# The last network's second weight as a scaled pair of fp16 parts, in four of five chunks

## The chip, the cores and the metric

The kernel is one program on one core of a Trainium2 chip. The metric is the device time of one execution in microseconds (us). The core has five engines with a queue each that is worked through strictly in order: PE (matrix products), DVE (vector), ACT (scalar functions), POOL (GpSimd) and SP (here it issues DMAs); they meet through semaphores only. Matrix products write to PSUM, everything else lies in SBUF.

## The reference

```python
attn = softmax(causal(q @ k.T / 8 + decay(f))) @ v          # 4 x 8 heads, 576 tokens, 64 wide
h = relu(attn @ w_in);  u, v = halves(h)                    # first network: 512 -> 2 x 512
x = (u * (w_spatial @ layernorm(v) + b_spatial)) @ w_out    # "moe"
xk = mu_k * x + (1 - mu_k) * previous_token(x)              # last network: "moe2"
xr = mu_r * x + (1 - mu_r) * previous_token(x)
k = relu(xk @ w_k)                                          # 512 -> 1024
out = sigmoid(xr @ w_r) * ((k * k) @ w_v)                   # 1024 -> 512
```

All is float32 with 2304 tokens in all. The weights arrive as 8-byte numbers and are converted to float32 on the chip.

## The kernel before, in words

Every float32 operand of a product is cut into a high and a low part, and a product is three matrix multiplications (`T3`: high x high, high x low, low x high) that add up in PSUM. Most operands are cut into **scaled fp16 parts**: a power of two is found from the operand's size (squares on ACT, a sum over all partitions by a small product with a matrix of ones on PE, named `tot`, and a few one-column instructions on DVE in `pow2`), ACT multiplies and rounds to the high part, and one SCALAR_TENSOR_TENSOR on DVE makes the low part. The second weight of the last network (`moe2_w_v`) and its operand, the squares `k2`, are cut without a scale into **two fp32r parts** (`split`: an ACT cast, a DVE subtraction).

The first 395 us are attention and the first network. What follows is the stage of the change: the 2304 tokens in five chunks (four of 512, the last of 256). Chunk by chunk there are, on PE, with names as in the code and line 927 of `mm` for all of them:

- `m3`: 4 groups of 12 matmuls (w_out), for the next chunk; ACT writes `x2` (L897), POOL copies one column across the chunk's edge (L899);
- `mix`: no PE; ACT (L947, L957) and DVE (L949, L958) make the fp16 parts `xx0`, `xx1` of xk and xr;
- `m4(fc)`, fc 0 to 7: 12 matmuls each (w_k, fp16); then ACT takes the relu out of PSUM (L976), DVE squares it (L977), ACT and DVE cut the square into fp32r parts (L65, L66);
- `m5(fc)`: 12 matmuls (4 groups of 128 tokens x 3), w_v as the moving operand, `k2` as weights, adding into four PSUM banks over all eight fc;
- `m6(j)`: 12 matmuls for each group of 128 tokens (w_r, fp16); ACT takes the sigmoid (L996).

At the end DVE multiplies the sums by the sigmoids (L1002) and SP writes the result out (L1004). Within `chunk`, m5 runs two steps behind m4: m4(fc), m5(fc-2); then the four m6, then m5(6) and m5(7). m4, m3, m6 and the `tot` products share four PSUM banks.

The order in each engine's queue is not the order of the code: a scheduler with a timing model of its own lays the queues out when the program is built, so a change of code moves instructions of several engines. `side` in `body` hands the next chunk's m3 and mix in between the steps of a chunk; `wrest` does the same with the loading and converting of weights.

Of the kernel before, what the change touches and what calls it, by code (L numbers as in the profile page):

```python
# [7 lines left out]
F32 = mybir.dt.float32  # L8
# [31 lines left out]
def f32(ap):  # L40
    return ap.bitcast(F32)


class K:
# [705 lines left out]
    def early_norms(self):  # L750

        nc, p = self.nc, self.p3
        self.ws = self.p3.tile([128, 4], F32, name="ws")
        wq = p.tile([128, 2, 4], F32, name="wq")
        self.gate_load(0)
        for n, nm in enumerate(("moe2_w_k", "moe_w_out")):
            for kc in range(4):
                self.sumsq(wq[:, n, kc:kc + 1], self.we[nm, kc, 0], self.junk2[:, 0:512])
                if kc % 2:
                    yield  # L760
        for x in range(2):
            self.gate_sums(0, x)
        self.gate_load(1)
        yield
        for x in range(2):
            self.gate_sums(1, x)
        yield
        w = p.tile([128, 2], F32, name="wt")
        nc.vector.tensor_reduce(w, self.total(wq.rearrange("p n k -> p (n k)"), 8).rearrange("p (n k) -> p n k", n=2), AX.X, ALU.add)
        with self.tc.high_priority(PRIO):  # L770
            self.pow2(self.ws[:, 0:2], w, 1e-12, 15)
            self.gsum(0)
            self.mixing_norms()
            self.gsum(1)
        yield
# [29 lines left out]
    def weights2(self, p, names, stage, pin=False):  # L805
# [5 lines left out]
        blocks = []  # L811
        for nm in names:
            rows, cn = a[nm].shape
            self.w2[nm] = p.tile([128, 2, rows // 128, cn], F16 if nm in SCALED else F32R, name=nm)
            blocks += [(nm, kc, slice(c0, c0 + 512)) for c0 in range(0, cn, 512) for kc in range(rows // 128)]

        ready = [x for x in blocks if (x[0], x[1], x[2].start) in self.we]
# [133 lines left out]
    def mix_parts(self, i, w, kc):  # L951
# [5 lines left out]
        nc.scalar.mul(hi, tmp[:, 0:n], sc)  # L957
        nc.vector.scalar_tensor_tensor(self.xx[w][:, 1, kc, 0:n], tmp[:, 0:n], sc, hi, ALU.mult, ALU.subtract)  # L958

    def chunk(self, i):  # L960
        nc, p = self.nc, self.p2
        t0, n = self.chunks[i]
        xk, sx = self.xx[0], self.sx3[i]
        wk, wr, wv = [self.w2["moe2_w_" + x] for x in "krv"]
# [5 lines left out]
        def m4(fc):  # L970
            ps = self.ps3.tile([128, 512], F32, tag="p", bufs=4, name="m4")
            self.mm(ps[:, 0:n], [(wk[:, ws, kc, 128 * fc:128 * fc + 128], xk[:, s_, kc, 0:n]) for kc in range(4) for s_, ws in T3])
            tmp = p.tile([128, 512], F32, tag="tmp", bufs=3, name="tmp")
            t = k2[fc] = p.tile([128, 2, 512], F32R, tag="k2", bufs=4, name="k2")
            u = 2 + 2 * (fc // 4)
            nc.scalar.activation(tmp[:, 0:n], ps[:, 0:n], AF.Relu, scale=sx[:, u:u + 1])  # L976
            nc.vector.tensor_tensor(tmp[:, 0:n], tmp[:, 0:n], tmp[:, 0:n], ALU.mult)  # L977
# [23 lines left out]
        for j in range(J):  # L1001
            nc.vector.tensor_tensor(o[j], o[j], acc[j], ALU.mult)  # L1002
            r0 = t0 + 128 * j
            nc.sync.dma_start(self.out.rearrange("b s d -> (b s) d")[r0:r0 + 128, :], o[j])  # L1004
        yield


def body(tc, a, out):
# [66 lines left out]
    for w in range(2):  # L1075
        for _ in k.mix(0, w):
# [2 lines left out]
            k.late_part()  # L1079
            next(wrest, 0)  # L1080
    for i in range(5):
        lg = k.gates(i + 2) if i < 2 else iter(())
        side = (x for y in ((m3[i + 1], k.mix(i + 1, 0), k.mix(i + 1, 1)) if i < 4 else ()) for x in y)
        n = 0
        for _ in k.chunk(i):
            if not i:
                k.late_part()
            next(wrest, 0)
            n += 1
            if n > 5:  # L1090
                next(lg, 0)
            if n <= 5 and i or n >= 9:
                next(side, 0)
            if n == 12:
                next(side, 0)
        for _ in side:
            next(wrest, 0)
    for p in (k.ps3, k.p2, wst, k.p3, wp, k.hl, k.c):
        p.release()


# [42 lines left out]
```

## Time and profile before

| | |
|---|---|
| median of 3 runs | 692.7 us (687.59, 692.7, 693.89) |
| the profiled execution's own time | 688.2 us |
| its span, first to last instruction | 686.5 us |
| busy: PE, DVE, ACT, POOL | 90%, 63%, 67%, 28% |
| mean granted TensorE clock | 0.981 |

The busy share is an average over stages; the span in 40 slices shows PE filled to nine tenths or more in nearly every slice after the first few, and POOL busy in the first half alone. Times in the trace count from the span's first instruction. A matmul's duration in the trace overlaps with the next one's: the price of one in a stream is the step from start to start.

### The profile page before, as it was taken

The page shows a single profiled execution, that of the slowest core. Times are in us where ns is not written, and L with a number is a line of the kernel's source. Part 1 is how long each engine was busy: PE and PEld are TensorE (multiplying, and loading weights), DVE is VectorE, ACT ScalarE, POOL GpSimd, SP SyncE. Part 2 cuts the span into 40 slices and gives each one's busy share as a digit, 9 for nine tenths or more (in the row PEclk, how much of TensorE's full clock was granted, in tenths as well). Part 3 has the DMA queues.
Part 4 walks back from the last instruction along what each step waited for, and adds up shares of the span by engine and source line. Part 5 has one row for each costly group of instructions (what it writes and reads, how often), then busy time and mean ns, then how long its engine had stood idle before and what let it go on. Part 6 is the DMA issues. An engine that isn't in the chain of part 4 may idle for free.

```text
span 686.5 us, 11120 instructions
## 1 busy us (share of the span) xinstructions
PE 616.0 (90%) x3720; PEld 368.8 (54%) x3720; DVE 435.8 (63%) x1238; ACT 462.4 (67%) x1022; POOL 189.7 (28%) x421
## 2 busy tenths in 40 slices
PE   0458686998988999989999799999999999999997
PEld 0123343566645566456667544565555556566584
DVE  6776857888578866685237978997328624532341
ACT  4678899898879978689339699885328334442531
POOL 7343444665446743475106010000000000000000
PEclk9998789999999999999999999999999999999999
DMA  7984632826763455441046582313001100100010
GB/s 236 233 220 105 166 87 59 233 48 165 191 143 106 109 138 128 103 90 32 19 146 213 178 283 70 123 62 123 0 1 32 62 1 0 62 1 0 1 62 32
DMA packets 69344, 69.75 MB, mean 102 GB/s; under 512 B 46659, under 2 KB 47395, under 8 KB 69286
## 3 DMA queue, kind: packets, MB, share of 16 engines
q1 hardware_dynamic: 68854, 67.85, 35.3%
q10 hardware_dynamic: 432, 1.18, 0.4%
q8 instruction: 29, 0.48, 0.3%
q14 instruction: 29, 0.24, 0.1%
HBM read 43.61 MB, written 9.55 MB: 77 GB/s over the span
## 4 chain that ended last, share of the span: by engine, by line
PE 66%; DVE 12%; DMA 10%; ACT 4%; SPq 3%; POOL 3%; issue 2%; DVEq 0%; POOLq 0%; ACTq 0%
PE m L927 42%; PE m L615 5%; PE o L393 4%; PE t L352 4%; PE s L298 4%; PE m1u L598 4%; DVE sx L309 3%; DMA qA<-qT 3%; PE m1v L530 3%; DMA qT<-nq 2%; SPq L341 2%; ACT junka L321 1%; DMA wst<-in_moe_w_k_dram 1%; DMA kT<-nk 1%; DMA qA<-mr 1%
## 5 line engine op out<-in xcount | busy, mean ns | idle before, releaser
L321 ACT ACTIVATE junka<-sx,nb,qa 128x576 bf16<-128x576 f32 (+4 forms) x160 | 103.7, 648 | 22.4 <-POOL nb L318 19.1
L927 PE MATMUL m<-moe_w_v,k 128*128 128x512 f32 x432 | 111.9, 407 | 0.0
L927 PE MATMUL m<-xx,moe_w_k 128*128 128x512 f16 (+1 forms) x480 | 99.1, 358 | 0.0
L927 PEld LDWEIGHTS m<-moe_w_v,k 128*128 128x128 f32 x432 | 80.8, 188 | 19.5
L309 DVE CUSTOM_DVE_ANT_0 sx<-s,mask 128x512 f32<-128x512 f32 (+4 forms) x160 | 72.4, 473 | 25.3 <-PE s L298 20.1
L298 PE MATMUL s<-kT,qT 128*128 128x512 f16 (+2 forms) x192 | 55.8, 310 | 29.6 <-DVE nm L309 10.8
L362 ACT ACTIVATE e<-t,qa 128x512 f32<-128x512 f32 x96 | 64.0, 680 | 21.5 <-PE t L352 21.3
L927 PEld LDWEIGHTS <-moe_w_k 128*128 128x128 f16 x480 | 45.5, 98 | 46.7 <-issue 5.0
L366 POOL TENSOR_SCALAR_AFFINE_SELECT e<-e 128x128 f32<-128x128 f32 x128 | 47.1, 380 | 84.1 <-ACT e L362 83.4
L976 ACT ACTIVATE tmp<-m,sx 128x512 f32<-128x512 f32 (+1 forms) x40 | 25.8, 644 | 56.2 <-PE m L927 56.2
L977 DVE TENSOR_TENSOR tmp<-tmp 128x512 f32<-128x512 f32 (+1 forms) x40 | 25.5, 637 | 57.6 <-ACT tmp L976 57.6
L393 PE MATMUL o<-e,v 128*64 128x64 f32 (+4 forms) x384 | 55.1, 407 | 5.4 <-DVE mr L339 1.4
L298 PE MATMUL s<-kA,qA 67*128 67x512 f16 (+2 forms) x192 | 49.2, 308 | 9.6 <-DMA qA<-qT 6.4
L615 PE MATMUL m<-wspT,vn 128*128 128x288 f16 x384 | 54.9, 286 | 0.1
L899 POOL COPY x<-x 128x1 f32<-128x1 f32 x16 | 4.1, 270 | 183.5 <-ACT x L897 174.4
L927 PE MATMUL m<-gh,moe_w_out 128*128 128x512 f16 (+1 forms) x240 | 50.6, 367 | 3.5 <-DVE u L618 3.5
L598 PE MATMUL m1u<-xt,win 128*128 128x288 f16 x384 | 52.5, 286 | 0.4 <-ACT vt L550 0.4
L352 PE MATMUL t<-qA,kA 70*128 70x512 f16 (+2 forms) x192 | 49.1, 293 | 3.6 <-DMA qA<-mr 3.3
L352 PE MATMUL t<-qT,kT 128*128 128x512 f16 (+2 forms) x192 | 50.9, 292 | 0.0
L530 PE MATMUL m1v<-win,xt 128*128 128x512 f16 x192 | 49.2, 389 | 0.3 <-ACT xt L396 0.3
L927 PE MATMUL m<-moe_w_r,xx 128*128 128x512 f16 x216 | 48.8, 379 | 0.0
L949 DVE SCALAR_TENSOR_TENSOR mt<-x,mu,mt 128x64 f32<-128x64 f32 (+4 forms) x64 | 30.2, 515 | 26.5 <-ACT mt L947 25.9
(218 smaller groups left out, 1136.1 us busy)
## 6 DMA issues: line engine op xcount, KB each, us to landing
knat<-in_k_dram SPq DMA_DIRECT2D x16, 320.0 KB
v<-in_v_dram SPq DMA_DIRECT2D x20, 256.0 KB
gd<-u SPq DMA_DIRECT2D x16, 288.0 KB
gl<-gd SPq DMA_DIRECT2D x8, 576.0 KB
out_dram<-o SPq DMA_DIRECT2D x18, 256.0 KB
qnat<-in_q_dram SPq DMA_DIRECT2D x14, 320.0 KB
wst<-in_moe_w_k_dram SPq DMA_DIRECT2D x8, 512.0 KB
g<-gd SPq DMA_DIRECT2D x16, 256.0 KB
```

The costliest lines, as they stand in the source:

```text
L298: self.nc.tensor.matmul(s[:, o:o + n], self.tok(qn, p, h, 128 * ib - 64, 128)[0:r], self.tok(kn, p, h, k0, n)[0:r], start=(j == 0), stop=( ...
L309: self.nc.vector.tensor_tensor_reduce(out=self.sx[g][r0:, SO[ib] + k0:SO[ib] + k0 + n], in0=self.s[u % 2][r0:, o:o + n], in1=self.mask[r0: ...
L321: self.nc.scalar.activation(self.junka[r, 0:n], self.sx[g][r, SO[ib]:SO[ib] + n], AF.Exp, scale=qa[r, 5:6], bias=nb[r, i:i + 1], accum_out ...
L352: self.nc.tensor.matmul(t[:, o:o + n], self.tok(kn, p, h, 128 * c, 128)[0:r], self.tok(qn, p, h, q0, n)[0:r], start=(j == 0), stop=(j == 1))
L362: self.nc.scalar.activation(self.e[g][:, 512 * u:512 * u + 512], t, AF.Exp, scale=self.qa[p][:, 5:6])
L366: self.nc.gpsimd.affine_select(out=e, in_=e, pattern=[[1, 128]], compare_op=ALU.is_ge, fill=0.0, base=0, channel_multiplier=-1)
L393: self.chain(self.nc.tensor.matmul(o[r, 448 + f:448 + q1], v[:, c, pr, r], e, start=(c == 0), stop=(c == 4 or q1 == 64)))
L530: nc.tensor.matmul(self.m1p, xt[:, xs, 128 * j:128 * j + 128], self.win[:, ws, kc, 512:1024], **flags)
L598: self.nc.tensor.matmul(o, self.win[:, ws, kc, fs], self.xt[(4 * b + kc) % 8][:, xs, ts_], start=(kc == 0 and n == 0), stop=(kc == 3 and n ...
L615: nc.tensor.matmul(o, pairs[n][0], pairs[n][1], start=(n == 0), stop=(n == 13))
L927: self.nc.tensor.matmul(out, l, r, start=(first and j == 0), stop=(last and j == len(pairs) - 1))
L949: nc.vector.scalar_tensor_tensor(tmp[:, r0:r1], x2[:, kc, r0:r1], self.mu[:, w, 1, kc:kc + 1], tmp[:, r0:r1], ALU.mult, ALU.add)
```

## The change

For chunks 1 to 4 the product with w_v is made of scaled fp16 parts. Chunk 0 stays as it was. New are:

- `value_norm`: eight sums of squares of w_v's high parts on ACT, one `tot` product on PE, a scale in `ws[:, 4]`.
- `value_parts`: for each of the eight blocks, POOL adds w_v's two fp32r parts back together into `e` (2 buffers), ACT and DVE cut the sum into fp16 parts `w16`. Both run as `parts` between the steps of chunk 1, two steps at a time.
- `chunk16`: all eight m4 first; DVE squares and takes the largest element in one instruction (tensor_tensor_reduce); then the four m6; after the first of them `kscale` finds the squares' scale (two small DVE instructions, a `tot` product on PE, six more small ones on DVE); `ksplit` cuts the squares into fp16 parts; then all m5. At the end a SCALAR_TENSOR_TENSOR undoes the scales.

The first weight stage's buffers are given back before chunk 1, and a new pool (`phase4`) takes their place for eight unsplit squares; `tmp` and `k2` of chunk 0 move to a pool `phase6`. The next chunk's mix begins after step 12 of a chunk instead of step 8.

```diff
--- before.py
+++ after.py
@@ -750,7 +750,7 @@
     def early_norms(self):
 
         nc, p = self.nc, self.p3
-        self.ws = self.p3.tile([128, 4], F32, name="ws")
+        self.ws = self.p3.tile([128, 6], F32, name="ws")
         wq = p.tile([128, 2, 4], F32, name="wq")
         self.gate_load(0)
         for n, nm in enumerate(("moe2_w_k", "moe_w_out")):
@@ -811,7 +811,8 @@
         blocks = []
         for nm in names:
             rows, cn = a[nm].shape
-            self.w2[nm] = p.tile([128, 2, rows // 128, cn], F16 if nm in SCALED else F32R, name=nm)
+            if nm not in self.w2:
+                self.w2[nm] = p.tile([128, 2, rows // 128, cn], F16, name=nm)
             blocks += [(nm, kc, slice(c0, c0 + 512)) for c0 in range(0, cn, 512) for kc in range(rows // 128)]
 
         ready = [x for x in blocks if (x[0], x[1], x[2].start) in self.we]
@@ -957,8 +958,33 @@
         nc.scalar.mul(hi, tmp[:, 0:n], sc)
         nc.vector.scalar_tensor_tensor(self.xx[w][:, 1, kc, 0:n], tmp[:, 0:n], sc, hi, ALU.mult, ALU.subtract)
 
+    def value_norm(self):
+
+        wv = self.w2["moe2_w_v"]
+        q = self.p3.tile([128, 8], F32, name="vq")
+        for fc in range(8):
+            self.sumsq(q[:, fc:fc + 1], f32(wv[:, 0, fc]), self.junk2[:, 0:512])
+            yield
+        self.nc.vector.tensor_reduce(self.ws[:, 5:6], self.all_sum(q, 8), AX.X, ALU.add)
+        self.pow2(self.ws[:, 4:5], self.ws[:, 5:6], 1e-12, 15)
+
+    def value_parts(self):
+
+        nc, wv, sc = self.nc, self.w2["moe2_w_v"], self.ws[:, 4:5]
+        self.wv16 = {}
+        for fc in range(8):
+            e = self.p6.tile([128, 512], F32, tag="e", bufs=2, name="ev")
+            nc.gpsimd.tensor_tensor(e, f32(wv[:, 0, fc]), f32(wv[:, 1, fc]), ALU.add)
+            w = self.wv16[fc] = self.p6.tile([128, 2, 512], F16, name=f"w16{fc}")
+            nc.scalar.mul(w[:, 0], e, sc)
+            nc.vector.scalar_tensor_tensor(w[:, 1], e, sc, w[:, 0], ALU.mult, ALU.subtract)
+            yield
+
     def chunk(self, i):
         nc, p = self.nc, self.p2
+        if i:
+            yield from self.chunk16(i)
+            return
         t0, n = self.chunks[i]
         xk, sx = self.xx[0], self.sx3[i]
         wk, wr, wv = [self.w2["moe2_w_" + x] for x in "krv"]
@@ -970,8 +996,8 @@
         def m4(fc):
             ps = self.ps3.tile([128, 512], F32, tag="p", bufs=4, name="m4")
             self.mm(ps[:, 0:n], [(wk[:, ws, kc, 128 * fc:128 * fc + 128], xk[:, s_, kc, 0:n]) for kc in range(4) for s_, ws in T3])
-            tmp = p.tile([128, 512], F32, tag="tmp", bufs=3, name="tmp")
-            t = k2[fc] = p.tile([128, 2, 512], F32R, tag="k2", bufs=4, name="k2")
+            tmp = self.p6.tile([128, 512], F32, tag="tmp", bufs=3, name="tmp")
+            t = k2[fc] = self.p6.tile([128, 2, 512], F32R, tag="k2", bufs=4, name="k2")
             u = 2 + 2 * (fc // 4)
             nc.scalar.activation(tmp[:, 0:n], ps[:, 0:n], AF.Relu, scale=sx[:, u:u + 1])
             nc.vector.tensor_tensor(tmp[:, 0:n], tmp[:, 0:n], tmp[:, 0:n], ALU.mult)
@@ -1003,6 +1029,71 @@
             r0 = t0 + 128 * j
             nc.sync.dma_start(self.out.rearrange("b s d -> (b s) d")[r0:r0 + 128, :], o[j])
         yield
+
+    def chunk16(self, i):
+
+        nc, p = self.nc, self.p2
+        t0, n = self.chunks[i]
+        xk, sx = self.xx[0], self.sx3[i]
+        wk, wr = [self.w2["moe2_w_" + x] for x in "kr"]
+        J = n // 128
+        acc, o, kk, kp = [], [], {}, {}
+        self.unscale(i, 2, 4)
+        kx = self.p4.tile([128, 16], F32, tag="kx", bufs=2, name="kx")
+
+        def m4(fc):
+            ps = self.ps3.tile([128, 512], F32, tag="p", bufs=4, name="m4")
+            self.mm(ps[:, 0:n], [(wk[:, ws, kc, 128 * fc:128 * fc + 128], xk[:, s_, kc, 0:n]) for kc in range(4) for s_, ws in T3])
+            t = kk[fc] = self.p4.tile([128, 512], F32, tag="kk", bufs=8, name="kk")
+            u = 2 + 2 * (fc // 4)
+            nc.scalar.activation(t[:, 0:n], ps[:, 0:n], AF.Relu, scale=sx[:, u:u + 1])
+            nc.vector.tensor_tensor_reduce(out=t[:, 0:n], in0=t[:, 0:n], in1=t[:, 0:n], op0=ALU.mult, op1=ALU.max, scale=1.0, scalar=0.0, accum_out=kx[:, fc:fc + 1])
+
+        def kscale():
+            v = nc.vector
+            v.tensor_scalar(kx[:, 0:8], kx[:, 0:8], 2.0 ** -40, None, op0=ALU.mult)
+            v.tensor_tensor(kx[:, 0:8], kx[:, 0:8], kx[:, 0:8], ALU.mult)
+            v.tensor_reduce(kx[:, 8:9], self.all_sum(kx[:, 0:8], 8), AX.X, ALU.add)
+            self.pow2(kx[:, 9:10], kx[:, 8:9], 1e-12, 15)
+            v.tensor_tensor(kx[:, 10:11], kx[:, 9:10], self.ws[:, 4:5], ALU.mult)
+            self.inv2(kx[:, 11:12], kx[:, 10:11])
+
+        def ksplit(fc):
+            t = kp[fc] = self.p4.tile([128, 2, 512], F16, tag="k2", bufs=4, name="k2")
+            nc.scalar.mul(t[:, 0, 0:n], kk[fc][:, 0:n], kx[:, 9:10])
+            nc.vector.scalar_tensor_tensor(t[:, 1, 0:n], kk[fc][:, 0:n], kx[:, 9:10], t[:, 0, 0:n], ALU.mult, ALU.subtract)
+
+        def m5(fc):
+            for j in range(J):
+                if fc == 0:
+                    acc.append(self.ps3.tile([128, 512], F32, tag=f"a{j}", bufs=1, name=f"m5_{j}"))
+                self.mm(acc[j], [(kp[fc][:, s_, 128 * j:128 * j + 128], self.wv16[fc][:, ws]) for s_, ws in T3], fc == 0, fc == 7)
+
+        for fc in range(8):
+            m4(fc)
+            yield
+        xr = self.xx[1]
+        for j in range(J):
+            pr = self.ps3.tile([128, 512], F32, tag="p", bufs=4, name="m6")
+            self.mm(pr, [(xr[:, s_, kc, 128 * j:128 * j + 128], wr[:, ws, kc]) for kc in range(4) for s_, ws in T3])
+            o.append(p.tile([128, 512], F32, tag="o", bufs=4, name="o"))
+            nc.scalar.activation(o[j], pr, AF.Sigmoid, scale=sx[:, 5:6])
+            if j == 0:
+                with self.tc.high_priority(PRIO):
+                    kscale()
+            for fc in range(4 * j // J, 4 * (j + 1) // J):
+                ksplit(fc)
+            yield
+        for fc in range(8):
+            m5(fc)
+            if fc < 4:
+                ksplit(fc + 4)
+            if fc == 7:
+                for j in range(J):
+                    nc.vector.scalar_tensor_tensor(o[j], acc[j], kx[:, 11:12], o[j], ALU.mult, ALU.mult)
+                    r0 = t0 + 128 * j
+                    nc.sync.dma_start(self.out.rearrange("b s d -> (b s) d")[r0:r0 + 128, :], o[j])
+            yield
 
 
 def body(tc, a, out):
@@ -1067,6 +1158,8 @@
         yield from w2c
         yield from w2b
     wrest = rest()
+    k.w2["moe2_w_v"] = k.p2.tile([128, 2, 8, 512], F32R, name="moe2_w_v")
+    k.p6 = k.pool("phase6", side="left")
     m3 = {i: k.m3(i) for i in range(5)}
     for n, _ in enumerate(m3[0]):
         next(wrest, 0)
@@ -1079,6 +1172,14 @@
             k.late_part()
             next(wrest, 0)
     for i in range(5):
+        if i == 1:
+            for _ in wrest:
+                pass
+            wst.release()
+            k.p6.release()
+            k.p4 = k.pool("phase4", side="right")
+            k.p6 = k.pool("phase6", side="left")
+            parts = (x for g in (k.value_norm(), k.value_parts()) for x in g)
         lg = k.gates(i + 2) if i < 2 else iter(())
         side = (x for y in ((m3[i + 1], k.mix(i + 1, 0), k.mix(i + 1, 1)) if i < 4 else ()) for x in y)
         n = 0
@@ -1089,13 +1190,16 @@
             n += 1
             if n > 5:
                 next(lg, 0)
-            if n <= 5 and i or n >= 9:
+            if i == 1:
+                for _ in range(2):
+                    next(parts, 0)
+            if n <= 5 and i or n >= (13 if i else 9):
                 next(side, 0)
-            if n == 12:
+            if n == 12 and not i:
                 next(side, 0)
         for _ in side:
             next(wrest, 0)
-    for p in (k.ps3, k.p2, wst, k.p3, wp, k.hl, k.c):
+    for p in (k.ps3, k.p6, k.p2, k.p4, k.p3, wp, k.hl, k.c):
         p.release()
 
 
```

Three places show how the queues change. On **PE**, before, within chunk 1: names like m_0 to m_3 are the four sums of m5, the m with a number of its own is m4 (moe_w_k) or m3 (moe_w_out).

```order
L927 MATMUL m_5680<-xx_5420,moe_w_k 128x512
L927 MATMUL m_0_5649<-moe_w_v,k_5610 128x512 x3
L927 MATMUL m_1_5653<-moe_w_v,k_5610 128x512 x3
L927 MATMUL m_2_5657<-moe_w_v,k_5610 128x512 x3
L927 MATMUL m_3_5661<-moe_w_v,k_5610 128x512 x3
L927 LDWEIGHTS moe_w_out
L927 MATMUL m_5711<-gh,moe_w_out 128x512
```

After each 12 matmuls of m4, 12 of m5 stood; now no m5 stands among the m4, and where chunk 1 has come to its m6 the queue reads:

```order
L928 MATMUL m_5840<-moe_w_r,xx_5496 128x512
L717 MATMUL tot<-kx,ones 128x8
L928 LDWEIGHTS xx_5496
L928 MATMUL m_5868<-moe_w_r,xx_5496 128x512
```

The `tot` product of kscale stands right behind the 12 matmuls of the first m6, and the second m6 behind it; so it is in chunks 2, 3 and 4.

On **DVE**, chunk 1, from the parts of w_v's sixth block (w_5809) to the first instruction that reads `tot`; ISA kk,kx is the square with its largest element, and ISA kx the instruction that writes that out; xx_5948 belongs to chunk 2's mix.

```order
L980 SCALAR_TENSOR_TENSOR w_5809<-ev,ws,w_5809 128x512
L980 SCALAR_TENSOR_TENSOR w_5832<-ev,ws,w_5832 128x512
L1050 ISA kk,kx<-kk 128x512
L1050 ISA kx 128x1
L959 SCALAR_TENSOR_TENSOR xx_5948<-mt,sx,xx_5948 128x512
L1054 TENSOR_SCALAR kx<-kx 128x8
L959 SCALAR_TENSOR_TENSOR xx_5948<-mt,sx,xx_5948 128x512
L1055 TENSOR_TENSOR kx<-kx 128x8
L959 SCALAR_TENSOR_TENSOR xx_5948<-mt,sx,xx_5948 128x512
L980 SCALAR_TENSOR_TENSOR w_5837<-ev,ws,w_5837 128x512
L1056 TENSOR_REDUCE kx<-tot 128x1
```

Seven of the eight weight parts now stand ahead of the last square, and two parts of the next chunk's mix between that square and what `tot` waits for.

On **POOL**, from the end of the first network on:

```order
-L899 COPY x_5568<-x_4886 128x1 x4
-L899 COPY x_6040<-x_5568 128x1 x4
+L900 COPY x_5580<-x_4890 128x1 x4
+L977 TENSOR_TENSOR ev<-moe_w_v 128x512 x2
+L900 COPY x_6115<-x_5580 128x1 x3
+L977 TENSOR_TENSOR ev<-moe_w_v 128x512
+L900 COPY x_6115<-x_5580 128x1
+L977 TENSOR_TENSOR ev<-moe_w_v 128x512 x5
```

POOL had only copies of one column left in this stage; now eight additions of 512 columns stand among those of chunk 2's m3. SP issues the same DMAs in the same order.

## Rows read from the trace of the kernel before

**Rows 1.** The page's chain that ended last, shares of the span by engine.

```profile
PE 66%; DVE 12%; DMA 10%; ACT 4%; SPq 3%; POOL 3%; issue 2%; DVEq 0%; POOLq 0%; ACTq 0%
```

**Rows 2.** Busy time by stretch: from:to length, engines (instructions), clock, DMA share, GB/s.

```profile
540.00:560.00 20.00, 20.00 (x92) 11.17 (x91) 6.24 (x12) 7.68 (x12) 0.55 (x3) 1.00 0.00 0
```

**Rows 3.** Timeline of PE in chunk 2: start, length, instruction, output and inputs, count.

```profile
522.52 0.28 PE L717 MATMUL tot<-gq,ones 128*128 128x4 f32 x2
522.66 5.34 PE L927 MATMUL m<-moe_w_r,xx 128*128 128x512 f16 x24
...
533.33 5.35 PE L927 MATMUL m<-xx,moe_w_k 128*128 128x512 f16 x24
538.52 2.75 PE L927 MATMUL m<-gh,moe_w_out 128*128 128x512 f16 x12
541.11 2.75 PE L927 MATMUL m<-xx,moe_w_k 128*128 128x512 f16 x12
543.52 3.10 PE L927 MATMUL m<-moe_w_v,k 128*128 128x512 f32 x12
546.45 2.76 PE L927 MATMUL m<-gh,moe_w_out 128*128 128x512 f16 x12
549.05 2.75 PE L927 MATMUL m<-xx,moe_w_k 128*128 128x512 f16 x12
```

**Rows 4.** Timeline of ACT and DVE there, behind the last m4.

```profile
543.90 0.69 ACT L976 ACTIVATE tmp<-m,sx 128x512 f32<-128x512 f32 x1 [1.09 <-PE m L927]
544.62 0.69 DVE L977 TENSOR_TENSOR tmp<-tmp 128x512 f32<-128x512 f32 x1 [0.83 <-ACT tmp L976]
```

**Rows 5.** Groups by line and shape, 395 us to end: count | busy, mean ns | idle before.

```profile
L958 DVE SCALAR_TENSOR_TENSOR xx<-mt,sx,xx 128x512 f16<-128x512 f32 x32 | 23.1, 747 | 7.4 <-ACT xx L957 7.3
L957 ACT ACTIVATE xx<-mt,sx 128x512 f16<-128x512 f32 x32 | 21.6, 714 | 3.3 <-DVE mt L949 3.3
L958 DVE SCALAR_TENSOR_TENSOR xx<-mt,sx,xx 128x256 f16<-128x256 f32 x8 | 3.5, 479 | 8.3 <-ACT xx L957 8.3
L922 DVE TENSOR_TENSOR sx<-sx,ws 128x1 f32<-128x1 f32 x18 | 2.2, 154 | 0.1
```

**Rows 6.** Groups by line and shape of DVE, whole span: square-like instruction, its accumulator.

```profile
L309 DVE CUSTOM_DVE_ANT_0 sx<-s,mask 128x512 f32<-128x512 f32 x32 | 22.0, 688 | 11.9 <-PE s L298 8.2 <-ACT junka L321 2.4 <-ACT e L362 1.1
...
L309 DVE DVE_READ_ACCUMULATOR2_ANT nm<- 128x1 f32 x160 | 12.9, 81 | 0.0
```

**Rows 7.** Timeline of POOL and DVE: an undisturbed cast, then one among DVE's parts.

```profile
365.60 0.61 POOL L578 CAST vn<-v 128x512 f16<-128x512 f32 x1
...
376.53 0.94 POOL L575 CAST v<-vt 64x512 f16<-64x512 f32 x1 [1.51 <-DVE vt L573]
376.92 1.09 DVE L832 SCALAR_TENSOR_TENSOR moe_w_out<-emoe_w_out,ws,moe_w_out 128x512 f16<-128x512 f32 x1
...
379.02 0.73 DVE L832 SCALAR_TENSOR_TENSOR moe_w_out<-emoe_w_out,ws,moe_w_out 128x512 f16<-128x512 f32 x1
```

**Rows 8.** Timeline of PE, 386 to 399 us: the last idle time before the stage.

```profile
393.55 5.73 PE L927 MATMUL m<-gh,moe_w_out 128*128 128x512 f16 x18 [3.52 <-DVE u L618]
```

**Rows 9.** Busy time by stretch, columns as in rows 2.

```profile
394.00:396.00 2.00, 2.00 (x8) 0.80 (x7) 0.50 (x2) 0.50 (x1) 0.00 (x0) 0.65 1.01 292
396.00:398.00 2.00, 2.00 (x6) 0.69 (x5) 2.00 (x7) 1.54 (x5) 0.00 (x0) 0.50 1.00 364
```

**Rows 10.** Timeline of the end: DVE behind the last m5.

```profile
681.61 1.37 DVE L1002 TENSOR_TENSOR o<-o,m 128x512 f32<-128x512 f32 x2 [6.80 <-PE m L927]
```

**Rows 11.** Groups by line and shape, 395 us to end: products and their weight loads.

```profile
L927 PE MATMUL m<-moe_w_v,k 128*128 128x512 f32 x432 | 111.9, 407 | 0.0
...
L927 PEld LDWEIGHTS m<-moe_w_v,k 128*128 128x128 f32 x432 | 80.8, 188 | 19.5
L927 PE MATMUL m<-moe_w_r,xx 128*128 128x512 f16 x216 | 48.8, 379 | 0.0
...
L927 PEld LDWEIGHTS <-xx 128*128 128x128 f16 x216 | 20.5, 98 | 25.6 <-issue 2.7
```

## The prediction

> **What bounds the kernel now.** I read the chain of waits first, since only work on it can shorten the time: PE holds 66% of it [rows 1]. Then the busy time by stretch, for the stage that the change touches, since a share over the whole span mixes stages: in chunk 2's 20 us PE is busy for all 20.00, at a granted clock of 1.00, with DVE at 6.24, ACT at 7.68, POOL at 0.55 [rows 2]. In that stage PE alone sets the pace. Two things follow. What PE is spared comes off the time in full; and every wait put on PE is added in full, since PE has no idle time to absorb it.
>
> Last the timeline of PE, for the price of one matmul, start to start [rows 3]. 24 fp16 matmuls of m4 take 538.52 - 533.33 = 5.19 us, 0.216 each. The round from 541.11 to 549.05 is 12 of m4, 12 of m5 (fp32r) and 12 of m3, 7.94 us; less 5.19 for the 24 fp16 ones, the 12 of m5 cost 2.75, or 0.229 each.
>
> **The matmuls.** Chunks 1 to 4 hold 14 groups of 128 tokens, 8 fc and 3 products each: 336 matmuls, 28 blocks of 12. In fp16 a block costs 2.59 instead of 2.75: **-4.5 us** (28 x 0.16). m6 has the very form that m5 gets, fp16 512 columns wide, and runs at that step [rows 3].
>
> **The new sums on PE.** A `tot` delays the next product by 522.66 - 522.52 = 0.14 us [rows 3]. There are five more: **+0.7**.
>
> **The wait of kscale.** This is new: PE meets a `tot` behind the first m6, and all later products are queued behind it. It needs the largest squares of m4(7). Count from the first m6's start, when the last m4 matmul has begun 0.216 earlier. In rows 3 and 4 ACT starts 543.90 - 543.52 = 0.38 after the next block's first start, which lies about 0.19 early in the record (the step before it is short, 2.41 for 12), so ACT starts some 0.2 after m6 does. The relu takes 0.69, the hand-over to DVE 0.03 [rows 4], the square with its largest element 0.69 [rows 6]. DVE's queue then has a part of xx0, a small one, a part, a small one: 0.75 and 0.15 [rows 5], less 0.08 overlap each. That is 0.2 + 0.69 + 0.03 + 0.69 + 2 x 0.67 + 2 x 0.08 + 0.1 = 3.2 us, against 12 x 0.216 = 2.6 of m6. PE stands for about 0.6 in chunks 1 and 2; in chunk 3 three parts of half the width (0.48 [rows 5]) make it 0.5. In chunk 4 all lies narrower and no mix is left: nothing. For chunks 2 and 3 together **+1.1**. The splitting that follows (8 x 0.71 on ACT, 8 x 0.75 on DVE, by the rows of L957 and L958 [rows 5]) lies beside three more m6 (7.8 us) and m5; the first m5 needs one part only. If that cover went, its price would be the first part, about 1.5 us a chunk.
>
> **Chunk 1 has a second load, w_v's new parts.** The eight squares on ACT and the `tot` lie beside m4. The chain that matters begins at that `tot`: from it to the `tot` of kscale PE has 12 m3, 36 m4 and 12 m6, 60 x 0.216 + 0.14 = 13.1 us. DVE can begin with the parts about 2.5 us in (four small ones, a square, ACT's first part 0.71). Then its queue holds, up to what kscale's `tot` waits for, 7 parts of w_v and 2 of xx0 at 0.67 net, 3 squares at 0.62 net (688 - 73 of overlap, its accumulator hidden the same way [rows 6]), 2 small ones: 8.1. End at 10.6, before PE gets there; by this the wait stays at the 0.6 above.
>
> But seven of POOL's eight additions must come before those parts too. Two can be ready early (two buffers), so five fall inside. And POOL and DVE get in each other's way: a SCALAR_TENSOR_TENSOR of the same form takes 0.73 alone and 1.09 when it meets a POOL cast, and the cast 0.94 instead of 0.61 [rows 7]. So I add their times instead of overlapping them. The Trainium skill (SBUF — State Buffer, "Who interferes with whom") says that a DVE instruction with two SBUF inputs contends with a GpSimd instruction that reads SBUF, as one lock held for the instruction; the rows 7 agree in kind, though the part waited 0.36 of the cast's remaining 0.55, not all of it. By a lock the two add up; with free ports the term below would stay at 0.6.
>
> No row shows an addition of 512 columns on POOL. Bounds from the cast: 0.61, if a second input is free, and 1.9, twice the disturbed 0.94. I take 1.2, twice the undisturbed cast, since two inputs of that size are read. (The Trainium skill, GPSIMD Engine Reference, "Performance versus the Vector engine", has 4497 ns for 2048 columns; an estimate from that is 1.1, and the sum would be 0.5 lower.) Then DVE ends at 10.6 + 5 x 1.2 = 16.6, and PE waits 16.6 - 13.1 = **+3.5**. Ends: at 0.61, 13.65, a wait of 0.6; at 1.9, 20.1, a wait of 7.0.
>
> **Edits at nothing.** SP issues the same DMAs in the same order. POOL's copies for chunk 2's m3 stand behind additions now; who needs them is chunk 2's mix, 20 us later. Chunk 0's m5 stand a few matmuls earlier among its m4; that costs nothing while PE stays filled. At the end SCALAR_TENSOR_TENSOR replaces the product [rows 10], 0.75 against 0.68: **+0.1**.
>
> **Sum.** -4.5 + 0.7 + 1.1 + 3.5 + 0.1 = **+0.9**. Made against the profiled execution, 688.2 (span 686.5 and 1.7 around it), that is 689.1. That execution lies 4.5 under the median of the runs, which themselves reach from 687.6 to 693.9; against the median the forecast is 692.7 + 0.9, **693.6 us**.
>
> **Rivals.**
>
> - *The ports do not matter* (the additions lie beside DVE): chunk 1 waits 0.6 as chunk 2 does, the sum is -2.0, 690.7. For it: DVE runs at a third in such a stretch before [rows 2], and the part in rows 7 did not wait to the cast's end. Against it: in chunk 1 the squares and both kinds of parts fill most of the time. Chance 0.28.
> - *Slower: POOL's additions carry chunk 1.* At 1.9 each the wait is 7.0. And PE standing long loses its clock: after 3.52 us without work [rows 8] the granted clock was 0.65, then 0.50, which is the 1.2 of the two levels 1.2 and 2.4 GHz [rows 9], and 18 matmuls took 5.57 (5.73 less the last one's overlap) instead of 3.89, +1.7. Together -4.5 + 0.7 + 1.1 + 7.0 + 1.7 + 0.1 = +6.1, 698.8. The total turns positive from an addition of 1.0 us on; a loss of over 1% (6.9) with the clock needs a wait of 7.8, an addition of 2.1. At my forecast's 3.5 the clock may already fall, giving +2.6. Chance 0.18, a third of it beyond 1%.
> - *Faster: the weight loads count.* Busy time by group gives m5 111.9 / 432 = 0.259 each against 48.8 / 216 = 0.226 for m6, and its loads 188 ns against 98 [rows 11]. If that 0.033 were the price, 336 x 0.033 = 11.1 would go instead of 4.5: 687.0, and with no wait of the ports 684.1. The Trainium skill (TensorE: Matmul & The Clock Gate, "Weight-path perf modes") says that weights other than fp32 load faster, which by itself would favour this. Against it: a load of 188 lies within the step of 229, and the group's mean counts the overlap with the other products' records. Chance 0.07.
> - *The step does not change* (512 columns either way, and the 0.013 has another cause): +5.4, 698.1. m6's step speaks against it. Chance 0.05.
>
> The forecast has 0.40, with its clock variant; 0.02 is left for what I do not see.
>
> **Numbers.** What a measurement of this kernel can tell from no change is about 1%, 6.9 us. Faster than 685.8: half of the weight-load case, and a little of the first rival should the runs fall at the low end of their spread (687.6 - 2.0 = 685.6): 0.07. Slower than 699.6: a third of the POOL case and the edge of the unchanged step: 0.09. Within 1%: 0.84. The range takes in the first rival at the runs' low end and the POOL case at 1.9: 686 to 699.
>
> **What would show it.** In the profile after: 12 matmuls of m5 in 2.59 us; PE idle before the line of the `tot` in the first m6 of chunks 1 to 3, some 3.5, 0.6 and 0.5 us, released by DVE; POOL's additions of 1.2 us and more, and in chunk 1 DVE parts and squares longer than 0.75 and 0.69. I am wrong if the step stays at 0.229, if chunk 1's wait is as short as chunk 2's, or if PE stands elsewhere, as at the first m5 of a chunk.

## The result, and the profile after

The changed kernel takes 696.4 us (median of 10 runs) against 691.9 for the kernel before (10 runs): a ratio of 1.0059, 95% interval 1.0031 to 1.0088, or +2.1 to +6.1 us. The forecast was +0.9 us and 693.6; the time lies in its range of 686 to 699, above its middle. That range is 13 us wide and holds the times of all four rivals too (687.0, 690.7, 698.1, 698.8), so the time alone settles nothing between them.

The profiled execution is one of the longer ones, 701.0 us (span 699.3, clock 0.971), and only part of that is the change. The time ahead of the second stage varies from execution to execution. So I measure the stage by itself, from the first `tot<-wq` on PE (behind m3 of chunks 0 and 1) to the end of the span. The later runs stand in the same table, with one trace for each kernel:

| kernel | `tot<-wq` at | span | stage | against before |
|---|---|---|---|---|
| before | 415.95 | 686.48 | 270.53 | |
| changed | 423.52 | 699.32 | 275.80 | +5.27 |
| additions on DVE | 419.10 | 691.76 | 272.67 | +2.14 |
| POOL only writes | 421.52 | 690.98 | 269.45 | -1.08 |
| additions early | 425.05 | 693.81 | 268.75 | -1.78 |
| early, late scale | 413.82 | 682.37 | 268.55 | -1.98 |
| early, late scale but in the last chunk | 419.42 | 686.27 | 266.85 | -3.68 |
| new order alone, fp32r | 417.56 | 689.92 | 272.36 | +1.83 |
| each addition twice | 421.03 | 696.62 | 275.59 | +5.06 |

The first column moves by 11 us from execution to execution, so neither it nor the span can be used for differences of a few us. The stage is steadier: chunk 0 with its scales, up to the first m3 behind it, is the same work in all nine kernels and takes 58.7 to 59.1 us. A difference of less than 0.4 us between two stages says nothing until its place in the trace is found. The change is worth +5.27 us in its own stage, which the interval of the medians holds.

Where does it come from? First the waits of PE in the changed kernel from 390 us on (what waited, on what, total, times, longest):

```profile
PE tot L717 <- ACT o L1080: 4.2, 1, 4.2
PE m L928 <- DVE u L618: 3.5, 1, 3.5
PE tot L717 <- DVE kx L1055: 0.5, 1, 0.5
PE tot L717 <- ACT mt L948: 0.4, 1, 0.4
```

The 3.5 is the one of [rows 8]; the three others are new, each at a `tot` of kscale, in chunks 1, 2 and 3. The timeline of PE shows the first in its place:

```profile
498.09 0.28 PE L717 MATMUL tot<-vq,ones 128*128 128x8 f32 x2
498.23 2.75 PE L928 MATMUL m<-gh,moe_w_out 128*128 128x512 f16 x12
500.82 7.93 PE L928 MATMUL m<-xx,moe_w_k 128*128 128x512 f16 x36
508.59 2.75 PE L928 MATMUL m<-moe_w_r,xx 128*128 128x512 f16 x12
515.59 0.56 PE L717 MATMUL tot<-kx,ones 128*128 128x8 f32 x2 [4.25 <-ACT o L1080]
516.01 5.28 PE L928 MATMUL m<-moe_w_r,xx 128*128 128x512 f16 x12
521.08 0.43 PE L717 MATMUL tot<-gq,ones 128*128 128x4 f32 x2
521.37 5.46 PE L928 MATMUL m<-moe_w_r,xx 128*128 128x512 f16 x24
...
528.61 16.57 PE L928 MATMUL m<-w,k 128*128 128x512 f16 x76
```

From the `tot` of w_v's scale (`tot<-vq`) to PE's arrival at kscale's (`tot<-kx`) the products take 498.09 to 511.18 (508.59 + 12 x 0.216), the 13.1 us of the prediction; the `tot` starts at 515.59, 4.41 later. Then 12 matmuls of m6 take 516.01 to 521.08, 5.07 us instead of 2.59. The busy time by stretch tells why (columns as in [rows 2]):

```profile
510.00:512.00 2.00, 1.34 (x7) 0.39 (x4) 1.76 (x2) 1.01 (x2) 1.37 (x2) 1.00 0.00 0
512.00:514.00 2.00, 0.00 (x0) 0.00 (x0) 2.00 (x4) 2.00 (x4) 0.85 (x1) 1.00 0.01 4
514.00:516.00 2.00, 0.41 (x2) 0.44 (x3) 2.00 (x6) 2.00 (x5) 0.00 (x0) 0.70 0.01 4
516.00:518.00 2.00, 2.00 (x6) 0.72 (x7) 2.00 (x8) 1.37 (x3) 0.00 (x0) 0.50 0.03 8
518.00:520.00 2.00, 2.00 (x6) 0.76 (x5) 1.38 (x4) 0.49 (x1) 0.00 (x0) 0.50 0.00 0
...
522.00:524.00 2.00, 2.00 (x11) 0.89 (x10) 1.88 (x12) 1.61 (x4) 0.00 (x0) 1.00 0.00 0
```

Behind the idle time the granted clock is 0.50, the 1.2 of 1.2 and 2.4 GHz, as in [rows 9], and it is back by 522. In the two stretches from 512 to 516, in which PE stands nearly all the time, DVE is busy for 2.00 of 2.00 us. DVE, with POOL beside it, is where to look. The profile names ACT's `o` as the releaser, but that sigmoid ended at 515.31; the small DVE instruction of kscale, 515.33 to 515.49, came last.

The timeline of DVE and of POOL in that stretch:

```profile
503.95 1.11 DVE L980 SCALAR_TENSOR_TENSOR w<-ev,ws,w 128x512 f16<-128x512 f32 x1 [1.91 <-ACT w L979]
504.99 0.68 DVE L1050 CUSTOM_DVE_ANT_0 kk<-kk 128x512 f32<-128x512 f32 x1
...
505.60 1.74 DVE L980 SCALAR_TENSOR_TENSOR w<-ev,ws,w 128x512 f16<-128x512 f32 x1
507.58 1.66 DVE L980 SCALAR_TENSOR_TENSOR w<-ev,ws,w 128x512 f16<-128x512 f32 x1 [0.24 <-ACT w L979]
...
509.77 1.74 DVE L980 SCALAR_TENSOR_TENSOR w<-ev,ws,w 128x512 f16<-128x512 f32 x1
511.75 1.65 DVE L980 SCALAR_TENSOR_TENSOR w<-ev,ws,w 128x512 f16<-128x512 f32 x1 [0.24 <-ACT w L979]
```

```profile
503.25 1.27 POOL L977 TENSOR_TENSOR ev<-moe_w_v 128x512 f32<-128x512 f32 x1
505.14 1.65 POOL L977 TENSOR_TENSOR ev<-moe_w_v 128x512 f32<-128x512 f32 x1 [0.63 <-DVE w L980]
507.42 1.27 POOL L977 TENSOR_TENSOR ev<-moe_w_v 128x512 f32<-128x512 f32 x1 [0.63 <-DVE w L980]
509.31 1.64 POOL L977 TENSOR_TENSOR ev<-moe_w_v 128x512 f32<-128x512 f32 x1 [0.63 <-DVE w L980]
511.59 1.26 POOL L977 TENSOR_TENSOR ev<-moe_w_v 128x512 f32<-128x512 f32 x1 [0.63 <-DVE w L980]
```

The addition at 505.14 meets a square and takes 1.65 instead of 1.27; the part behind the square meets that addition, which ends at 506.79, and takes 1.74 where it takes 0.75 alone; the next part meets the next addition. They take turns. The ends show it best: each of these five parts ends 0.54 to 0.56 us after the addition beside it (505.06 after 504.52, 507.34 after 506.79, and so on), however early the part had started. So a part waits for the whole addition, and some 0.2 of its 0.75 us can pass during the wait (0.75 - 0.55). The same holds for [rows 7]: that part ended at 378.01, the cast at 377.47, 0.54 earlier, so it too had waited for the cast's end. The 0.36 of the prediction is the 0.55 that was left less this 0.2, and no doubt follows from it. (The Trainium skill, SBUF — State Buffer, "Who interferes with whom", says that a DVE instruction with two inputs from SBUF contends with a GpSimd instruction that reads SBUF, and calls the shared ports an exclusive lock. This stretch agrees in size too.)

Last the step of m5, by groups of instructions, beside [rows 11]:

```profile
L928 PE MATMUL m<-w,k 128*128 128x512 f16 x336 | 73.2, 379 | 0.0
```

All 336 matmuls are there. In the timeline above 76 take (16.57 - 0.38 + 0.22) / 76 = 0.216 each, as forecast.

### The profile page after: what moved, and what is told of

Read it like the earlier page. It is cut to its first block, busy times and chain, and to the rows that moved or that the text cites. A ratio compares the mean times of both kernels' runs of the same rounds, so it can differ in the third digit from the quotient of the medians.

```text
span 699.3 us, 11251 instructions
## 1 busy us (share of the span) xinstructions
PE 621.4 (89%) x3730; PEld 346.1 (49%) x3730; DVE 452.4 (65%) x1314; ACT 474.7 (68%) x1046; POOL 199.8 (29%) x429
## 3 DMA queue, kind: packets, MB, share of 16 engines
q10 hardware_dynamic: 432, 1.18, 0.4%
## 4 chain that ended last, share of the span: by engine, by line
PE 59%; DVE 11%; DMA 11%; ACT 9%; POOL 3%; issue 3%; SPq 3%; DVEq 0%; POOLq 0%; ACTq 0%
PE m L928 34%; PE t L352 5%; PE o L393 5%; PE m L615 4%; PE m1u L598 4%; PE s L298 4%; DVE sx L309 3%; PE m1v L530 3%; DMA qT<-nq 3%; DMA wst<-in_moe_w_r_dram 2%; SPq L341 2%; DMA qA<-mr 1%; ACT junk L70 1%; DMA qA<-qT 1%; DMA wst<-in_moe_w_k_dram 1%
## 5 line engine op out<-in xcount | busy, mean ns | idle before, releaser
L928 PE MATMUL m<-xx,moe_w_k 128*128 128x512 f16 (+1 forms) x480 | 97.3, 358 | 0.1
L928 PE MATMUL m<-w,k 128*128 128x512 f16 x336 | 73.2, 379 | 0.0
L1049 ACT ACTIVATE kk<-m,sx 128x512 f32<-128x512 f32 (+1 forms) x32 | 20.2, 632 | 68.0 <-PE m L928 68.0
L393 PE MATMUL o<-e,v 128*64 128x64 f32 (+4 forms) x384 | 57.4, 420 | 4.2 <-DVE mr L339 2.6
L928 PEld LDWEIGHTS <-k 128*128 128x128 f16 x336 | 32.9, 98 | 39.6
L928 PE MATMUL m<-moe_w_r,xx 128*128 128x512 f16 x216 | 51.7, 394 | 0.0
L1050 DVE CUSTOM_DVE_ANT_0 kk<-kk 128x512 f32<-128x512 f32 (+1 forms) x32 | 20.1, 629 | 38.9 <-ACT kk L1049 38.9
L615 PEld LDWEIGHTS <-vn 128*128 128x128 f16 x384 | 37.1, 100 | 10.8 <-issue 0.4
```

The costliest lines, as they stand in the source:

```text
L393: self.chain(self.nc.tensor.matmul(o[r, 448 + f:448 + q1], v[:, c, pr, r], e, start=(c == 0), stop=(c == 4 or q1 == 64)))
L615: nc.tensor.matmul(o, pairs[n][0], pairs[n][1], start=(n == 0), stop=(n == 13))
L928: self.nc.tensor.matmul(out, l, r, start=(first and j == 0), stop=(last and j == len(pairs) - 1))
```

## Experiments

**The additions on DVE.**

```diff
-            nc.gpsimd.tensor_tensor(e, f32(wv[:, 0, fc]), f32(wv[:, 1, fc]), ALU.add)
+            nc.vector.tensor_tensor(e, f32(wv[:, 0, fc]), f32(wv[:, 1, fc]), ALU.add)
```

> The eight additions of w_v's halves run on DVE instead of POOL; nothing else differs from the changed kernel. Theory (POOL's additions and DVE's instructions with two inputs from SBUF take each other's time): nothing is left on POOL to share with, so DVE's queue in chunk 1 holds the 10.6 us of the prediction and five additions of some 0.65, 13.9, against 13.1 us of products: the wait at kscale's tot falls from 4.2 to 0.6 to 1.2 us, the block of m6 behind it runs at 0.216 and not at 0.427, DVE's parts of w_v come back from 1.38 to about 0.75 us, and the kernel gains 5 to 6 us on the changed one: some 690.5, 1.5 below the kernel before. Rival (DVE simply has too much work in chunk 1, POOL's part in it does not matter): with five to eight more instructions of 0.65 on DVE the wait grows to 7 us or more, and the kernel is 3 us slower than the changed one.

Measured: 693.84 us, ratio to before 1.0041 (1.0007 to 1.0074), stage +2.14. An addition takes 685 ns, and the parts are back at 746, as two rows of the instructions on that tile show (minimum, median, maximum in ns; first and last start):

```profile
L977 DVE TENSOR_TENSOR ev<-moe_w_v x8: 684/685/691, 477.1 to 504.4; 128x512 f32<-128x512 f32 x8
...
L980 DVE SCALAR_TENSOR_TENSOR w<-ev,ws,w x8: 744/746/752, 495.8 to 508.4; 128x512 f16<-128x512 f32 x8
```

PE's timeline at kscale's `tot`:

```profile
503.86 2.75 PE L928 MATMUL m<-moe_w_r,xx 128*128 128x512 f16 x12
509.31 0.36 PE L717 MATMUL tot<-kx,ones 128*128 128x8 f32 x2 [2.70 <-ACT mt L948]
509.53 4.44 PE L928 MATMUL m<-moe_w_r,xx 128*128 128x512 f16 x12
```

The wait fell from 4.4 to 2.9 us (509.31 less 506.45), not to the 0.6 to 1.2 that I expected, and the clock still fell, to 0.50 from 510 to 512: the 12 of m6 took 4.27 from start to start. So the stage gained 3.1 us on the changed kernel's, not 5 to 6. DVE's load tells why: from the `tot` of w_v's scale to kscale's its queue held 8 parts of w_v, 3 of xx0 and 6 additions, where I had counted 7, 2 and 5. Three more at 0.61 to 0.67 are the missing 1.9. So DVE's own load is a second limit, close behind the first: with more work on DVE the wait fell, which the rival excludes, but it did not vanish.

**POOL only writes.**

```diff
-            nc.gpsimd.tensor_tensor(e, f32(wv[:, 0, fc]), f32(wv[:, 1, fc]), ALU.add)
+            for _ in range(3):
+                nc.gpsimd.memset(e, 0.01)
```

> POOL's addition is replaced by three fills of the same tile, which write SBUF and read nothing (the values of w_v are left out of chunks 1 to 4); who waits for whom is as in the changed kernel, and POOL is busy for as long or longer. Theory (what costs is that POOL reads SBUF while DVE reads two inputs): DVE's parts of w_v fall from 1.38 to about 0.75 us although POOL is as busy, and the wait at kscale's tot falls from 4.2 to under 1.5 us. Rival (DVE waits for POOL to deliver each tile, the sharing is a side effect): the parts still start one POOL delivery apart, the wait stays at 4 us or more.

Measured (one run): 692.69 us, stage -1.08. On the tile of the sums, and PE's wait at chunk 1's `tot` of kscale:

```profile
L978 POOL MEMSET ev<- x24: 524/525/530, 479.3 to 509.2; 128x512 f32 x24
...
L981 DVE SCALAR_TENSOR_TENSOR w<-ev,ws,w x8: 743/748/752, 498.7 to 512.3; 128x512 f16<-128x512 f32 x8
```

```profile
PE tot L717 <- ACT xx L958: 0.8, 1, 0.8
```

POOL is busy longer for each tile than in an undisturbed addition (1.46 to 1.70 us from the start of its three fills to their end, in place of 1.27), who waits for whom is the same, and no part is longer than 752 ns. The wait at kscale's `tot` is 0.94 us (a step of 1.157 less 0.216), and the m6 behind it runs at 0.216. The edit moved DVE's queue a little: 6 of the 8 parts stand before kscale's sums, 7 in the changed kernel. One part is 0.67 of the 3.5 us by which the wait fell, so the rest stands. Neither POOL's busy time nor the ring of two buffers made the long parts, but POOL's reading beside DVE's; the next run, which keeps the reading and moves it away in time, confirms it.

**The additions early.** Beside the squares, into eight buffers:

```diff
+        self.ev = {}
         for fc in range(8):
+            e = self.ev[fc] = self.p6.tile([128, 512], F32, tag="e", bufs=8, name="ev")
+            self.nc.gpsimd.tensor_tensor(e, f32(wv[:, 0, fc]), f32(wv[:, 1, fc]), ALU.add)
             self.sumsq(q[:, fc:fc + 1], f32(wv[:, 0, fc]), self.junk2[:, 0:512])
...
-            e = self.p6.tile([128, 512], F32, tag="e", bufs=2, name="ev")
-            nc.gpsimd.tensor_tensor(e, f32(wv[:, 0, fc]), f32(wv[:, 1, fc]), ALU.add)
+            e = self.ev[fc]
```

> The same eight additions on POOL, issued beside the squares (eight buffers for the sums), so that they run before the scale of w_v is known; the computation is the changed kernel's. Theory: DVE's parts of w_v no longer meet an addition and take 0.75 us, DVE is done at 10.6 us after the first tot, before PE gets there; the wait at kscale's tot in chunk 1 is 0.6 us as in chunk 2, its m6 runs at 0.216: 5.5 to 6.5 us less than the changed kernel, some 690.3. The additions meet DVE's work of chunk 0 instead, where PE has its operands well ahead: no new idle time of PE there. Rival (DVE's own load in chunk 1 is the limit): the wait stays above 3 us.

Measured: 691.05 us, ratio to before 0.996 (0.9925 to 0.9996), stage -1.78, 7.05 less than the changed kernel's (expected: 5.5 to 6.5 less). On the same tile, and PE's waits behind the one of [rows 8]:

```profile
L968 POOL TENSOR_TENSOR ev<-moe_w_v x8: 1261/1294/1722, 482.5 to 491.9; 128x512 f32<-128x512 f32 x8
...
L982 DVE SCALAR_TENSOR_TENSOR w<-ev,ws,w x8: 745/746/751, 501.9 to 506.5; 128x512 f16<-128x512 f32 x8
```

```profile
PE tot L717 <- DVE kx L1057: 0.5, 1, 0.5
PE tot L717 <- ACT xx L958: 0.4, 1, 0.4
PE tot L717 <- ACT mt L948: 0.4, 1, 0.4
```

Additions and parts no longer overlap in time. Counted from step to step, chunk 1's wait is 0.61, chunk 2's 0.65, chunk 3's 0.52: the theory's numbers. The rival, DVE's load by itself (squares and parts, without additions), falls.

**The scale behind the second m6.** As the last one, and:

```diff
-            if j == 0:
+            if j == 1:
                 with self.tc.high_priority(PRIO):
                     kscale()
-            for fc in range(4 * j // J, 4 * (j + 1) // J):
-                ksplit(fc)
+                for fc in range(4):
+                    ksplit(fc)
```

> As the run with the early additions, and kscale stands behind the second block of m6 instead of the first (the first four splits behind it). Theory: its tot has 2.6 us more of products ahead of it, more than the 0.5 to 0.6 us that PE waits in chunks 1 to 3, so these three waits go: 1.6 us less again, some 688.7, 3.2 below the kernel before (-4.5 for the step, +0.7 for the sums on PE, +0.1 at the end, some +0.5 for what else there is). Rival: the splits, which start 2.6 us later, bring the first m5 late: a wait there of 0.5 to 1.5 us in the last chunk, whose second m6 is its last, and the time is that of the run with the early additions.

Measured: 691.67 us where 688.7 was expected, ratio 0.9972 (0.9935 to 1.0009), stage -1.98, only 0.20 less than with the early additions. The three waits are gone, and the rival's came, near its upper end, before the first m5 of the last chunk:

```profile
665.38 0.28 PE L717 MATMUL tot<-kx,ones 128*128 128x8 f32 x2
667.03 10.53 PE L928 MATMUL m<-w,k 128*128 128x512 f16 x48 [1.36 <-ACT k L1065]
```

That chunk has two blocks of m6, so nothing lay between scale and first sum. (I had put that price at 1.5 us a chunk.)

**The same, but for the last chunk.** One more edit:

```diff
-            if j == 1:
+            if j == min(1, J - 2):
```

> As the run with the late scale, but in the last chunk (two blocks of m6 only) the scale stands behind the first block again. Theory: that chunk's wait of 1.4 us before its first m5 goes, no other comes; from the first tot of m3's weights to the end the stage takes 268.55 - 1.4 = 267.1 us against 270.53 before, -3.4, which is what is left of -4.5 for the step after +0.7 for five more sums on PE, +0.1 at the end and some +0.3. Rival: the scale behind the first m6 makes PE wait 0.5 us there, as in chunk 3: 267.7. The whole kernel: some 688, with the spread that lies in the part ahead of this stage.

Measured: 687.44 us against 691.58, ratio 0.9948 (0.9919 to 0.9976), stage -3.68 (266.85). PE's waits from 390 us on are down to one line, which is older than the change:

```profile
PE m L928 <- DVE u L618: 3.5, 1, 3.5
```

This version is faster than both kernels: by 0.5% (0.2 to 0.8) than the one before, and by the two ratios (0.9948 / 1.0059) by some 1.1% than the changed one, with which it was not measured side by side. The 0.5% is half of the 1% that the prediction took as what the median can tell; the stage, with no wait left in it, bears it out.

**The new order alone.** m5 stays in fp32r; without scale, scaled parts and new sums (the square without its largest element and the last product are as before, not printed here):

```diff
-                self.mm(acc[j], [(kp[fc][:, s_, 128 * j:128 * j + 128], self.wv16[fc][:, ws]) for s_, ws in T3], fc == 0, fc == 7)
+                self.mm(acc[j], [(kp[fc][:, s_, 128 * j:128 * j + 128], wv[:, ws, fc]) for s_, ws in T3], fc == 0, fc == 7)
...
-            t = kp[fc] = self.p4.tile([128, 2, 512], F16, tag="k2", bufs=4, name="k2")
-            nc.scalar.mul(t[:, 0, 0:n], kk[fc][:, 0:n], kx[:, 9:10])
...
+            t = kp[fc] = self.p4.tile([128, 2, 512], F32R, tag="k2", bufs=4, name="k2")
+            self.split(kk[fc][:, 0:n], t[:, 0, 0:n], t[:, 1, 0:n])
...
-                    kscale()
```

> The new order of chunks 1 to 4 (squares, gates, sums) alone: m5 stays in fp32r with the weight as it was, no scale, no scaled parts, no new sums on PE. Theory: the order costs nothing by itself and gives nothing, PE has no wait in the stage, and it takes 270.3 to 270.8 us from the first tot of m3's weights to the end, as before (270.53); what the fp16 step gives is then 4.5 us against this run. Rival (the step of 0.229 came from alternating m5 with other products, not from its form): with m5 in blocks of 48 and more the step falls toward 0.216 and the stage takes some 266 us.

Measured: 693.52 us, ratio 1.0022 (0.9993 to 1.005), stage +1.83. PE has no new wait. The rival is wrong in sign, and the theory, which gave the order no price, is wrong too. First this run, then a block of 24 of the kernel before:

```profile
507.67 5.34 PE L928 MATMUL m<-moe_w_r,xx 128*128 128x512 f16 x24
512.66 22.84 PE L928 MATMUL m<-moe_w_v,k 128*128 128x512 f32 x96
535.34 5.36 PE L928 MATMUL m<-xx,moe_w_k 128*128 128x512 f16 x24
```

```profile
527.65 5.84 PE L927 MATMUL m<-moe_w_v,k 128*128 128x512 f32 x24
```

With the first start corrected by the 0.19 by which it lies early (as in [rows 3]), 96 fp32r matmuls take 535.34 - 512.85 = 22.49 us, 0.234 each, against 0.229 in blocks of 12 between others, and as much in the block of 24 (533.33 - 527.84 = 5.49). From chunk 1's first m3 to the start of the last product PE takes 208.34 us against 206.95, +1.4; the other 0.4 of the 1.83 comes behind it, from the start of the last product to the end (5.12 against 4.68). In fp16 a block of 96 takes 20.72. So the prediction's -4.5 hides two opposite terms: fp32r in this version costs 1.4 more than before, and the fp16 form gives 6.2 in that order (3.5 blocks x 1.77).

That the order is the cause is not shown. The steps within a block speak against its length alone: from the tenth matmul on they are 0.226 to 0.227 in the block of 24, and 0.231 to 0.238 throughout the 96 here. This run also keeps the squares and their parts in another pool.

**Each addition twice.**

```diff
-            nc.gpsimd.tensor_tensor(e, f32(wv[:, 0, fc]), f32(wv[:, 1, fc]), ALU.add)
+            for _ in range(2):
+                nc.gpsimd.tensor_tensor(e, f32(wv[:, 0, fc]), f32(wv[:, 1, fc]), ALU.add)
```

> Each of POOL's additions is issued twice, all else is the changed kernel's. Theory (POOL's additions and DVE's parts take turns, so chunk 1's chain holds the five additions in full): the wait at kscale's tot in chunk 1 grows from 4.4 by 5 x 1.26 to some 10.7 us, and one part's time on DVE grows towards 1.9 to 3 us. Rival (an addition is partly beside other work): half of it is hidden and the wait is some 7.5 us.

Measured (one run): 698.34 us, stage +5.06, a wait of 4.4 as in the changed kernel: neither number. It is inconclusive, because the order of DVE's queue moved with the edit. Only 4 of the 8 parts stand before kscale's sums there, and 8 additions of 1.26 to 1.72 us fall before it in place of 6; the other parts follow later:

```profile
L978 POOL TENSOR_TENSOR ev<-moe_w_v x16: 1260/1421/1716, 478.5 to 519.8; 128x512 f32<-128x512 f32 x16
...
L981 DVE SCALAR_TENSOR_TENSOR w<-ev,ws,w x8: 735/742/1747, 497.8 to 526.8; 128x512 f16<-128x512 f32 x8
```

Two costs changed at once, so nothing follows on how much of an addition can be hidden. One thing does show: no part grew to the expected 1.9 us or more. The longest took 1.75 although two additions follow each other, so a part waits for the addition that is under way and not for the next one.

## Why the prediction was nearly right

- **The step of m5, -4.5.** Right: 0.216 for 336 matmuls. In size it was -4.8. From chunk 1's first m3 to the start of the last product the kernel before takes 206.95 us (474.85 to 681.80), the last version 202.89 (478.17 to 681.06), and 0.78 of new sums is in that: 4.06 + 0.78 = 4.84. The term hid an opposite pair (-6.2 and +1.4), which the new order in fp32r brought out.
- **Five more sums, +0.7.** Right: 0.14 each where nothing waits (681.25 to 681.39 in the changed kernel).
- **The tail, +0.1.** Too small. From the start of the last product to the end of the span it is 4.68 us before, 5.20 in the changed kernel and 5.12 in fp32r with the new order: +0.5, of which 0.4 has to do with the order and not with the new DVE instruction. Why is open. The last version's -3.68 is -0.14 in chunk 0, -4.06 and +0.53; that the forecast's terms also give -4.5 + 0.7 + 0.1 = -3.7 is luck, since an error of 0.3 and one of 0.4 nearly cancel.
- **kscale's wait in chunks 2 and 3, +1.1.** Measured 0.66 + 0.52 = 1.18 (steps of 0.872 and 0.735 less 0.216), nothing in chunk 4.
- **Chunk 1, +3.5.** The mechanism is the one forecast: POOL's additions and DVE's two-input instructions add up, shown by the ends of the parts (0.55 us after the addition's) and by the runs in which POOL only writes or adds early. The rival "the ports do not matter" falls. The size was 4.41. An addition takes 1.26, not 1.2, and the eighth got in ahead of the seventh part (511.59 against 511.75), so six fall inside, not five. I also left out a wait: the part on ACT lies between an addition and the part on DVE, so DVE stood idle for 1.91 and twice 0.24 us behind `w`, besides the 4.15 by which five of its parts were longer than 0.75 (1.11, 1.74, 1.66, 1.74, 1.65). Together 6.5 us in place of 5 x 1.2. That the two totals lie so near is partly luck: they are made of different pieces.
- **The clock, left out of the sum.** This is the step that was mis-sized most. I let PE stand for 3.5 us and kept the fast step behind it, and named the loss as a variant of +1.7, "the clock may already fall". [rows 8, 9] had shown it after 3.52 us. It fell, and cost 3.0: 2.48 in the 12 of m6 (5.07 - 2.59), 0.28 + 0.15 at two `tot`, 0.12 at the first product behind. But a row like [rows 8] is one draw: the same wait of 3.52 us ahead of the stage cost nothing in two of the nine traces (see the last section).
- **Sum.** For chunks 1 to 4, -4.84 + 0.7 + 1.18 + 4.41 + 3.03 and 0.16 for two more `tot` behind a wait (0.22 instead of 0.14) is 4.6, as measured (211.57 us against 206.95). With 0.13 in chunk 0 (-0.14, and 0.27 for a longer stop at the `tot<-wq` at 434.02, which three of the nine traces show in some length) and the tail's 0.52 that is the 5.27. The forecast had 0.9; the clock is 3.0 of the difference, chunk 1's wait 0.9, the tail 0.4, the step -0.3, and small pieces 0.4.
- The weight-load rival (an end at 687.0) falls: 0.014 a matmul was there to win (4.8 / 336), not 0.033. Whether the loads of 188 ns have a part in that 0.014 is not shown. The rival of the unchanged step falls too.

What stays open: why an fp32r step is 0.234 in the new order and 0.229 before, and why the tail grew by 0.4.

## What to carry to other kernels

Where a wait of several microseconds on a full PE is forecast, put the slower clock behind it into the sum with its chance, from rows of more than one trace, and not only into a variant. When work moves to an idle POOL, look at what DVE reads while POOL reads; work that needs no late operand belongs before the late operand is known. A new wait behind a short block of products is cheaper to cover by standing one block later than to shorten, but the stage's last and shortest round needs its own place for it.

## Behaviour of the chip that was not expected

- The clock after idle time of PE in this stage: 4.41 us without a product were followed by 0.50 for all 12 of m6; 2.86 us (additions on DVE) by a block of 4.27 instead of 2.59 us; 0.94 us (POOL only writes) by none of it.
- The clock does not fall behind every such wait. Ahead of the stage PE stands for 3.52 us in all nine traces (3.55 in one). In seven the clock fell after the first few products behind it; in two, with POOL only writing and with the late scale, it stayed at 1.00, and the 96 products of m3 took 20.88 us instead of 22.57. First the kernel before, then the late scale:

```profile
393.55 22.57 PE L927 MATMUL m<-gh,moe_w_out 128*128 128x512 f16 x96 [3.52 <-DVE u L618]
```

```profile
393.11 20.88 PE L928 MATMUL m<-gh,moe_w_out 128*128 128x512 f16 x96 [3.52 <-DVE u L618]
```

  The edits touch nothing ahead of these products, so the difference is one of the execution, worth 1.7 us. The 3.0 us behind the wait of 4.41 was the same in the second trace with such a wait (each addition twice); no other trace has one.
- An fp32r matmul of 512 columns costs 0.234 in blocks of 96 in the new order, 0.229 in the blocks of 12 and of 24 of the kernel before. No such difference shows for fp16: 0.216 in blocks of 12 and of 76.
- Beside POOL's fills, two-input instructions of DVE kept 0.75, but one small DVE instruction with one input waited: the TENSOR_SCALAR of 8 columns took 0.59 us in place of 0.16, and ended (509.79) with POOL's fill (509.77):

```profile
509.20 0.59 DVE L1055 TENSOR_SCALAR kx<-kx 128x8 f32<-128x8 f32 x1
...
509.94 0.16 DVE L1056 TENSOR_TENSOR kx<-kx 128x8 f32<-128x8 f32 x1
```

  The Trainium skill (SBUF — State Buffer, "Who interferes with whom") counts `tensor_scalar` among the instructions that can take the shared ports for reading and writing; this instance agrees with it. A second one, beside an addition instead of a fill, is in the run with each addition twice: 1.23 us, ended at 511.94, the addition at 511.91.
